# A fused FFT mixing and feed-forward kernel: its dense part put into program order on the compute engines, with a new order of issue

## The chip, the cores and the metric

One core of a Trainium2 chip. The metric is the device time of one launch in microseconds (us); lower is better. Each run of a kernel stands beside runs of the kernel before on the same chip, and all runs told here were in the fast state (no run was over 1.5% above the fastest of its kernel). The engines are named as in the profile: PE is TensorE, PEld its weight loads, DVE VectorE, ACT ScalarE, POOL GpSimd, SP SyncE.

## The reference

```python
def _attn_ref(x, filt_r, filt_i):                 # x: (8, 3008, 256)
    X = np.fft.rfft(x, axis=1)
    Y = X * (filt_r + 1j * filt_i)[None, :, :]
    return np.fft.irfft(Y, n=x.shape[1], axis=1).astype(np.float32)

def _moe_ref(x, w_in, w_out):                     # x: (24064, 256)
    h = x @ w_in                                  # 256 -> 2048
    g = h - np.tanh(h)
    return (g @ w_out).astype(np.float32)         # 2048 -> 256
```

The output of the first is the input of the second. Everything is fp32.

## The kernel before

A prologue transforms the first batch and prepares weights. Then comes the dense part: 48 groups of columns in five passes, each group in four *quarters*, 192 quarters in all. A quarter runs three stages at once, on different data: `up(U)` makes h for quarter U with seven half-size products in place of eight; `shrink(U-1)` turns h into h - tanh(h) by Arctan and Square, and makes four differences t on POOL; `down(U-2)` adds seven products into four accumulator banks. Between them run steps of the FFT of the next batch (`first`, `middle`: products pf, pz, pe). All eight PSUM banks are in use: x, y, z for `up`, t for the transforms, o0 to o3 for `down`.

```python
def up(U, between):
    ...
    mm(X, 1, True)
    s1 = copied("s1")                       # ACT copies bank x
    mm(Y, 2, True)
    between(0)
    V.tensor_add(h[:, 0, :, 0:w], Y, s1)
    mm(X, 6, False)                         # adds onto bank x: waits for the copy
    between(1)
    u2 = copied("u2")
    mm(Z, 5, True)
    between(2)
    mm(X, 7, False)
    u3 = copied("u3")
    between(3)
    V.tensor_add(h[:, 3, :, 0:w], Z, u3)
    mm(X, 4, False)
    between(4)
    V.tensor_copy(h[:, 2, :, 0:w], X)
    mm(Z, 3, False)                         # waits for the add above that reads bank z
    V.tensor_add(h[:, 1, :, 0:w], Z, u2)

def shrink(U):
    ...
    for k in (2, 0):                        # halves of h
        y[k], sq[k] = tiles("y", 2), tiles("sq", 1)
        ACT.activation(y[k], ht[k], AF.Arctan, scale=S)
        ACT.activation(y[k], y[k], AF.Square)
        yield
        V.tensor_mul(ht[k], ht[k], y[k])                       # "multiply"
        ACT.activation(sq[k], y[k], AF.Square, bias=near_b, scale=A)
        yield
        V.scalar_tensor_tensor(out=ht[k], in0=sq[k], scalar=K, in1=ht[k],
                               op0=ALU.add, op1=ALU.mult)      # "fused operation"
    t = dn.tile([128, 4, 2, 256], F32, tag="t", bufs=2, name="t")
    combine(blocks, [t[:, k, :, 0:w] for k in range(4)])       # four POOL subtractions
    ...

def down(U):
    ...
    mm(1, 2)
    if done:                                # last quarter of a group
        ACT.copy(p1, product(1))
        V.tensor_add(o[:, 0, 0:w], product(2), p1)
    yield
    ...                                     # mm(3, 5), mm(6, 7) likewise
    mm(4)
    if done:
        V.tensor_add(o[:, 1, 0:w], product(4), p1)
        store(i, o)                         # two DVE transposes, 32 stores

for U in range(total + 2):
    ...
    def between(k):
        if k < 4:
            next(dw, None)                  # a down step
        next(sh, None)                      # a shrink step
        ...                                 # transform steps that are due
```

Unless told otherwise, the program's scheduler reorders the instructions of each engine by its own simulated times; the order in the source is only a priority.

Of the kernel before, what the change touches and what calls it, by code (L numbers as in the profile page):

```python
# [22 lines left out]
NK = NQ // 2  # L23
# [11 lines left out]
XH = 2  # L35
# [10 lines left out]
def chunks_of(unit, size):  # L46
    n = steps_of(unit)
    return [(r, min(size, n - r)) for r in range(0, n, size)]
# [90 lines left out]
def kernel(  # L139
# [294 lines left out]

    hs, gs = {}, {}

    def up(U, between):

        i, u = divmod(U, 4)
        b, tu, w = uts[i]  # L440
        rhs = [b[0][0], b[1][0], b[1][1], tu[:, 3, 0:w], tu[:, 0, 0:w], tu[:, 1, 0:w],
               tu[:, 2, 0:w]]
        banks = {k: ps.tile([128, 2, 256], F32, tag=k, bufs=1, name=k) for k in "xyz"}
        X, Y, Z = (banks[k][:, :, 0:w] for k in "xyz")
        h = dn.tile([128, 4, 2, 256], F32, tag="h", bufs=3, name="h")
        hs[U] = (h, w)

        def mm(bank, q, first):
            for k in range(2):
                nc.tensor.matmul(bank[:, k], wu[:, q - 1, (2 * u + k) * 128:(2 * u + k + 1) * 128],  # L450
                                 rhs[q - 1], start=(first and k == 0), stop=True,
                                 skip_group_check=True)

        def copied(tag):
            t = dn.tile([128, 2, 256], F32, tag=tag, bufs=1, name=tag)[:, :, 0:w]
            ACT.copy(t, X)  # L456
            return t

        mm(X, 1, True)
        s1 = copied("s1")  # L460
        mm(Y, 2, True)
        between(0)
        V.tensor_add(h[:, 0, :, 0:w], Y, s1)  # L463
        mm(X, 6, False)
        between(1)
        u2 = copied("u2")
        mm(Z, 5, True)
        between(2)
        mm(X, 7, False)
        u3 = copied("u3")  # L470
        between(3)
        V.tensor_add(h[:, 3, :, 0:w], Z, u3)  # L472
        mm(X, 4, False)
        between(4)
        V.tensor_copy(h[:, 2, :, 0:w], X)  # L475
        mm(Z, 3, False)
        V.tensor_add(h[:, 1, :, 0:w], Z, u2)

    def shrink(U):

        h, w = hs.pop(U)
        ht = {k: h[:, k:k + 2].rearrange("p a b n -> p (a b) n")[:, :, 0:w] for k in (0, 2)}

        def tiles(tag, bufs):
            return dn.tile([128, 4, 256], F32, tag=tag, bufs=bufs, name=tag)[:, :, 0:w]

        y, sq = {}, {}
        for k in (2, 0):
            y[k], sq[k] = tiles("y", 2), tiles("sq", 1)
            ACT.activation(y[k], ht[k], AF.Arctan, scale=S)  # L490
            ACT.activation(y[k], y[k], AF.Square)  # L491
            yield
            V.tensor_mul(ht[k], ht[k], y[k])  # L493
            ACT.activation(sq[k], y[k], AF.Square, bias=near_b, scale=A)  # L494
            yield
            V.scalar_tensor_tensor(out=ht[k], in0=sq[k], scalar=K, in1=ht[k],  # L496
                                   op0=ALU.add, op1=ALU.mult)
        t = dn.tile([128, 4, 2, 256], F32, tag="t", bufs=2, name="t")
        blocks = [[h[:, 2 * a + k, :, 0:w] for k in range(2)] for a in range(2)]
        combine(blocks, [t[:, k, :, 0:w] for k in range(4)])  # L500
        gs[U] = (blocks, t, w)
        yield

    accs = {}

    def down(U):


        i, u = divmod(U, 4)
        b, t, w = gs.pop(U)  # L510
        rhs = [b[0][0], b[1][0], b[1][1], t[:, 3, :, 0:w], t[:, 0, :, 0:w], t[:, 1, :, 0:w],
               t[:, 2, :, 0:w]]
        if u == 0:
            accs[i] = [ps.tile([128, 2, 256], F32, tag=f"o{k}", bufs=1, name=f"o{k}")
                       for k in range(4)]
        acc = accs[i]
        at = {1: (0, 0), 2: (0, 1), 3: (1, 0), 5: (1, 1), 6: (2, 0), 7: (2, 1), 4: (3, 0)}

        def product(q):
            bank, k = at[q]  # L520
            return acc[bank][:, k, 0:w]

        def mm(*qs):
            for k in range(2):
                for q in qs:
                    nc.tensor.matmul(product(q), wd[:, q - 1, (2 * u + k) * 128:  # L526
                                                    (2 * u + k + 1) * 128],
                                     rhs[q - 1][:, k], start=(u == 0 and k == 0 and q == qs[0]),
                                     stop=(u == 3 and k == 1), skip_group_check=True)

        done = u == 3
        if done:
            p1, p5, u2, x12 = (dn.tile([128, 256], F32, tag=k, bufs=1, name=k)[:, 0:w]
                               for k in ("p1", "p5", "pu2", "x12"))
            o = dn.tile([128, 2, CH * 128], F32, tag="o", bufs=1, name="o")
        mm(1, 2)
        if done:
            ACT.copy(p1, product(1))
            V.tensor_add(o[:, 0, 0:w], product(2), p1)
        yield  # L540
        mm(3, 5)
        if done:
            ACT.copy(p5, product(5))
            V.tensor_add(x12, product(3), p5)
        yield
        mm(6, 7)
        if done:
            V.tensor_add(u2, product(6), p1)
            V.tensor_add(p1, product(7), u2)
            G.tensor_add(o[:, 0, w:2 * w], u2, x12)  # L550
            G.tensor_add(o[:, 1, w:2 * w], p1, p5)
        yield
        mm(4)
        if done:
            V.tensor_add(o[:, 1, 0:w], product(4), p1)
            accs.pop(i)
            store(i, o)
        yield

    def store(i, o):  # L560
# [116 lines left out]
    with tc.tile_pool(name="tr", bufs=2) as tr:  # L677
# [68 lines left out]
        with tc.tile_pool(name="dn", bufs=2) as dn, \  # L746
# [5 lines left out]
            for _ in last(0, z1):  # L752
                pass
            total = 4 * len(groups)
            for U in range(total + 2):
                i, u = divmod(U, 4)
                if U < total:
                    p, c = groups[i]
                    if c == 0 and u == 0:
                        units = 4 * len(CHUNKS[p])  # L760
                        steps, done = [], 0
                        if p + 1 < len(UNITS):
                            n_f = len(chunks_of(UNITS[p + 1], XH))
                            n_m = 2 * NK // (3 - len(UNITS[p + 1]))
                            steps = [(0.02 + 0.26 * k / n_f) * 4 * units for k in range(n_f)]
                            lo, hi = 0.34 * 4 * units, 4 * units - 14
                            steps += [lo + (hi - lo) * k / n_m for k in range(n_m)]
                            fs, ms = first(p + 1, z1), None
                    if u == 0 and i + 1 < len(groups) and c + 1 < len(CHUNKS[p]):
                        e2s[i + 1] = load_e2(*groups[i + 1])  # L770
                    if u == 2 and i + 1 < len(groups) and c + 1 == len(CHUNKS[p]):
                        e2s[i + 1] = load_e2(*groups[i + 1])
                    if u == 2 and i + 1 < len(groups):
                        lasts = last(i + 1, z1)
                sh = shrink(U - 1) if 0 <= U - 1 < total else iter(())
                dw = down(U - 2) if 0 <= U - 2 < total else iter(())

                def between(k):
                    nonlocal ms, done
                    if k < 4:  # L780
                        next(dw, None)
                    next(sh, None)
                    if U >= total:
                        return
                    if k < 4:
                        pos = 16 * c + 4 * u + k
                        while done < len(steps) and steps[done] <= pos:
                            if done < n_f:
                                next(fs)
                            else:  # L790
                                if ms is None:
                                    ms = middle(p + 1, z1)
                                next(ms)
                            done += 1
                    if u >= 2 and k in (1, 3) and i + 1 < len(groups):
                        next(lasts, None)
                    if i == len(groups) - 1 and k == 0:
                        next(bounds, None)

                if U < total:  # L800
                    if i == len(groups) - 1 and u == 0:
                        bounds = bounded(z1)
                    up(U, between)
                else:
                    for k in range(5):
                        between(k)

    within = nc.values_load(count[0:1, 0:1], min_val=0, max_val=128)
    with tc.If(within < 128):
# [33 lines left out]
```

## Time and profile before

| | before |
|---|---|
| time, median of 4 runs | 3037.57 us |
| prologue, dense part, tail | 206, 2807, 23 us |
| PE at its own spacing in the dense part | 2618 us |
| PE stalled in the dense part | 189 us |

The last two rows are the ones to read. The spacing is the distance from the start of one matmul record to the start of the next where nothing is waited for; whatever a distance is longer than that is a stall. Both are summed over the 12256 records of the dense part. Three rows of the costliest groups (line, engine, operation, tiles, shapes, count, then busy us, mean ns, and the idle time before):

```profile
L496 DVE SCALAR_TENSOR_TENSOR h<-sq,h 128x1024 f32<-128x1024 f32 (+2 forms) x384 | 474.7, 1236 | 181.5 <-ACT sq L494 175.5
L493 DVE TENSOR_TENSOR h<-h,y 128x1024 f32<-128x1024 f32 (+2 forms) x384 | 469.3, 1247 | 66.4 <-ACT y L491 64.1
...
L432 POOL TENSOR_TENSOR t<-t,h 128x512 f32<-128x512 f32 (+2 forms) x192 | 245.3, 1278 | 10.4
```

### The profile page before, as it was taken

What the parts mean: (1) busy time and instruction counts of PE and PEld (TensorE: products, weight loads), DVE (VectorE), ACT (ScalarE), POOL (GpSimd) and SP (SyncE); (2) the same over time, 40 slices, a digit from 0 to 9 for tenths busy, and PEclk for the clock granted to TensorE, in tenths of its full rate; (3) what the DMA queues carried; (4) which work ended last, traced back from release to release, by engine and by line L of the source; (5) the groups of instructions that cost most, each with busy time, mean ns of one, the idle gap of its engine ahead of it and who ended that gap; (6) DMA issues with size and microseconds to landing.
All of it is one profiled execution on the core that took longest, in us unless ns stands there. A gap on an engine that the chain in (4) does not pass through costs nothing.

```text
span 3035.6 us, 36258 instructions
## 1 busy us (share of the span) xinstructions
PE 2789.7 (92%) x12410; PEld 2261.0 (74%) x12410; DVE 1845.8 (61%) x2382; ACT 1822.8 (60%) x2432; POOL 1602.4 (53%) x1398
## 2 busy tenths in 40 slices
PE   2369999999999999999999999999999999999996
PEld 0247766887877777887877777788888878888886
DVE  4865565665655555665665565666666666666664
ACT  1336666666666666666666666656666666666563
POOL 4653676534465566554455565645455555544543
PEclk6569999999999999999999999999999999999998
DMA  9744343222222322222322222222122212110100
GB/s 165 268 119 131 98 117 109 80 75 80 74 69 57 76 78 60 65 61 83 86 58 61 69 74 61 69 60 61 44 50 57 73 46 51 32 27 14 21 8 15
DMA packets 328867, 220.32 MB, mean 73 GB/s; under 512 B 228305, under 2 KB 282581, under 8 KB 328322
## 3 DMA queue, kind: packets, MB, share of 16 engines
q1 hardware_dynamic: 272848, 151.84, 20.1%
q10 hardware_dynamic: 53202, 50.35, 5.5%
q0 software_dynamic: 2624, 15.73, 2.0%
q8 instruction: 100, 1.64, 0.2%
q14 instruction: 93, 0.76, 0.1%
HBM read 134.41 MB, written 83.36 MB: 72 GB/s over the span
## 4 chain that ended last, share of the span: by engine, by line
PE 76%; POOL 6%; ACT 5%; DVE 5%; DMA 4%; issue 3%; ACTq 0%; SPq 0%; POOLq 0%; DVEq 0%
PE o L526 32%; PE x L450 19%; PE z L450 9%; PE y L450 5%; PE pe L338 3%; PE pu L414 3%; PE pz L357 3%; POOL t L429 2%; PE pf L283 2%; DVE h L496 1%; POOL uv L374 1%; DMA ct<-a 1%; ACT sq L494 1%; DMA w<-in_moe_w_in_dram 1%; POOL o L550 1%
## 5 line engine op out<-in xcount | busy, mean ns | idle before, releaser
L526 PE MATMUL o<-t,wd 128*128 128x256 f32 (+2 forms) x3072 | 777.4, 375 | 0.5 <-POOL t L430 0.5
L429 POOL TENSOR_TENSOR t<-h 128x512 f32<-128x512 f32 (+2 forms) x192 | 239.3, 1246 | 847.0 <-DVE h L496 754.2
L526 PEld LDWEIGHTS o<-t,wd 128*128 128x128 f32 x3072 | 577.7, 190 | 77.9 <-issue 7.8
L490 ACT ACTIVATE y<-h 128x1024 f32<-128x1024 f32 (+2 forms) x384 | 385.1, 1032 | 384.4 <-DVE h L475 384.1
L450 PE MATMUL x<-tu,wu 128*128 128x256 f32 (+2 forms) x2304 | 593.8, 378 | 6.2 <-ACT u L456 6.0
L526 PE MATMUL o<-h,wd 128*128 128x256 f32 (+2 forms) x2304 | 585.5, 376 | 3.0 <-DVE h L496 2.9
L496 DVE SCALAR_TENSOR_TENSOR h<-sq,h 128x1024 f32<-128x1024 f32 (+2 forms) x384 | 474.7, 1236 | 181.5 <-ACT sq L494 175.5
L450 PEld LDWEIGHTS x<-tu,wu 128*128 128x128 f32 x2304 | 424.2, 190 | 157.2 <-issue 84.1
L493 DVE TENSOR_TENSOR h<-h,y 128x1024 f32<-128x1024 f32 (+2 forms) x384 | 469.3, 1247 | 66.4 <-ACT y L491 64.1
L526 PEld LDWEIGHTS o<-h,wd 128*128 128x128 f32 x2304 | 436.5, 191 | 60.0 <-DVE h L496 5.3
L494 ACT ACTIVATE sq<-y,near_b 128x1024 f32<-128x1024 f32 (+2 forms) x384 | 433.8, 1130 | 76.1 <-DVE h L496 71.6
L491 ACT ACTIVATE y<-y 128x1024 f32<-128x1024 f32 (+2 forms) x384 | 386.2, 1036 | 0.9
L456 ACT COPY u<-x 128x512 f32<-128x512 f32 (+2 forms) x384 | 219.7, 572 | 217.1 <-PE x L450 206.8
L463 DVE TENSOR_TENSOR h<-y,s 128x512 f32<-128x512 f32 (+2 forms) x192 | 130.3, 679 | 268.2 <-ACT s L456 206.2
L373 POOL TENSOR_TENSOR zs<-zs,ft 128x512 f32<-128x512 f32 x112 | 143.5, 1282 | 249.1 <-ACT zs L371 234.3
L450 PE MATMUL z<-ut,wu 128*128 128x256 f32 (+2 forms) x768 | 200.5, 382 | 65.2 <-DVE h L472 64.9
L432 POOL TENSOR_TENSOR t<-t,h 128x512 f32<-128x512 f32 (+2 forms) x192 | 245.3, 1278 | 10.4
L472 DVE TENSOR_TENSOR h<-z,u 128x512 f32<-128x512 f32 (+2 forms) x192 | 129.4, 674 | 194.9 <-ACT u L456 194.9
L430 POOL TENSOR_TENSOR t<-h,t 128x512 f32<-128x512 f32 (+2 forms) x192 | 239.7, 1249 | 0.0
L431 POOL TENSOR_TENSOR t<-h 128x512 f32<-128x512 f32 (+2 forms) x192 | 239.6, 1248 | 0.0
L450 PE MATMUL x<-ut,wu 128*128 128x256 f32 (+2 forms) x768 | 218.1, 408 | 11.1 <-DVE h L475 10.7
L450 PEld LDWEIGHTS z<-ut,wu 128*128 128x128 f32 x768 | 140.5, 190 | 100.8 <-DVE h L472 82.9
(96 smaller groups left out, 3360.5 us busy)
## 6 DMA issues: line engine op xcount, KB each, us to landing
a<-ct SPq DMA_DIRECT2D x64, 384.0 KB, 3.8
ct<-e ACTq DMA_DIRECT2D x128, 192.0 KB, 2.2
ft<-filt SPq DMA_DIRECT2D x48, 512.0 KB, 4.2
out_dram<-ot SPq DMA_DIRECT2D x1408, 16.0 KB, 1.5
x_sb<-in_x_dram SPq DMA_DIRECT2D x69, 256.0 KB, 2.8
ct<-a ACTq DMA_DIRECT2D x69, 256.0 KB, 2.7
e<-ct SPq DMA_DIRECT2D x33, 512.0 KB, 4.1
filt<-filt_sb POOLq DMA_DIRECT2D x2, 4096.0 KB, 16.1
```

Of the source, the lines that this page charges most:

```text
L429: G.tensor_sub(t[0], b[0][1], b[0][0])
L430: G.tensor_sub(t[1], b[1][1], t[0])
L431: G.tensor_sub(t[2], b[1][1], b[0][1])
L432: G.tensor_sub(t[3], t[1], b[1][0])
L450: nc.tensor.matmul(bank[:, k], wu[:, q - 1, (2 * u + k) * 128:(2 * u + k + 1) * 128], rhs[q - 1], start=(first and k == 0), stop=True, ski ...
L456: ACT.copy(t, X)
L490: ACT.activation(y[k], ht[k], AF.Arctan, scale=S)
L491: ACT.activation(y[k], y[k], AF.Square)
L493: V.tensor_mul(ht[k], ht[k], y[k])
L494: ACT.activation(sq[k], y[k], AF.Square, bias=near_b, scale=A)
L496: V.scalar_tensor_tensor(out=ht[k], in0=sq[k], scalar=K, in1=ht[k], op0=ALU.add, op1=ALU.mult)
L526: nc.tensor.matmul(product(q), wd[:, q - 1, (2 * u + k) * 128: (2 * u + k + 1) * 128], rhs[q - 1][:, k], start=(u == 0 and k == 0 and q == ...
```

## The change

Its intent: on each compute engine, work whose inputs are ready stands ahead of work that waits for a product of the running quarter; and PE, ACT, DVE and POOL then follow that order exactly (the program is told so by `tc.manual_schedule`; below this is called *forced*). Cut to its core:

```diff
-        mm(X, 1, True)
-        s1 = copied("s1")
-        mm(Y, 2, True)
-        between(0)
+        mm(X, 1, True)
+        mm(Y, 2, True)
+        s1 = copied("s1")
+        t(0); d(); s()                      # transform step, down products, shrink step
         V.tensor_add(h[:, 0, :, 0:w], Y, s1)
+        e(); s(); s(); t(1)                 # e: copies and adds of finished accumulators
         mm(X, 6, False)
-        between(1)
+        mm(Z, 5, True)
         u2 = copied("u2")
-        mm(Z, 5, True)
-        between(2)
+        d(); s(); e(); t(2)
         mm(X, 7, False)
         u3 = copied("u3")
-        between(3)
         V.tensor_add(h[:, 3, :, 0:w], Z, u3)
+        d(); s(); e(); t(3)
         mm(X, 4, False)
-        between(4)
         V.tensor_copy(h[:, 2, :, 0:w], X)
+        s(); d(); e(); t(4)
         mm(Z, 3, False)
         V.tensor_add(h[:, 1, :, 0:w], Z, u2)
@@ down
-            store(i, o)
+            stores.append((i, o))
@@ the loop over quarters
+            order = {nc.tensor.engine, ACT.engine, V.engine, G.engine}
+            with tc.manual_schedule(engines=order):
...
+                    def t(k):
+                        if k == 2 and stores:
+                            store(*stores.pop())      # one quarter later than before
...              # one transform step per slot, five slots per quarter
```

(Several calls are put on one line here; the shrink generator is split into six steps.)

More of the change, by code (lines that the diff above doesn't have):

```diff
@@ L435, with up @@
     hs, gs = {}, {}
-    def up(U, between):
+    def up(U, d, e, s, t):
         i, u = divmod(U, 4)
@@ L459, in up @@
         mm(X, 1, True)
+        mm(Y, 2, True)
         s1 = copied("s1")
-        mm(Y, 2, True)
-        between(0)
+        t(0)
+        d()
+        s()
         V.tensor_add(h[:, 0, :, 0:w], Y, s1)
+        e()
+        s()
+        s()
+        t(1)
         mm(X, 6, False)
-        between(1)
+        mm(Z, 5, True)
         u2 = copied("u2")
-        mm(Z, 5, True)
-        between(2)
+        d()
+        s()
+        e()
+        t(2)
         mm(X, 7, False)
         u3 = copied("u3")
-        between(3)
         V.tensor_add(h[:, 3, :, 0:w], Z, u3)
+        d()
+        s()
+        e()
+        t(3)
         mm(X, 4, False)
-        between(4)
         V.tensor_copy(h[:, 2, :, 0:w], X)
+        s()
+        d()
+        e()
+        t(4)
         mm(Z, 3, False)
@@ L487, in shrink, with start, square, end @@
         y, sq = {}, {}
-        for k in (2, 0):
-            y[k], sq[k] = tiles("y", 2), tiles("sq", 1)
+        def start(k):
+            y[k] = tiles("y", 2)
             ACT.activation(y[k], ht[k], AF.Arctan, scale=S)
             ACT.activation(y[k], y[k], AF.Square)
-            yield
+        def square(k):
+            sq[k] = tiles("sq", 1)
             V.tensor_mul(ht[k], ht[k], y[k])
             ACT.activation(sq[k], y[k], AF.Square, bias=near_b, scale=A)
-            yield
+        def end(k):
             V.scalar_tensor_tensor(out=ht[k], in0=sq[k], scalar=K, in1=ht[k],
                                    op0=ALU.add, op1=ALU.mult)
+        start(2)
+        yield
+        square(2)
+        yield
+        end(2)
+        yield
+        start(0)
+        yield
+        square(0)
+        yield
+        end(0)
         t = dn.tile([128, 4, 2, 256], F32, tag="t", bufs=2, name="t")
@@ L502, in shrink @@
         yield
-    accs = {}
+    accs, stores = {}, []
     def down(U):
@@ L536, in down @@
         mm(1, 2)
+        yield
         if done:
@@ L541, in down @@
         mm(3, 5)
+        yield
         if done:
@@ L546, in down @@
         mm(6, 7)
+        yield
         if done:
@@ L549, in down @@
             V.tensor_add(p1, product(7), u2)
+        yield
+        mm(4)
+        yield
+        if done:
+            V.tensor_add(o[:, 1, 0:w], product(4), p1)
             G.tensor_add(o[:, 0, w:2 * w], u2, x12)
             G.tensor_add(o[:, 1, w:2 * w], p1, p5)
-        yield
-        mm(4)
-        if done:
-            V.tensor_add(o[:, 1, 0:w], product(4), p1)
             accs.pop(i)
-            store(i, o)
+            stores.append((i, o))
         yield
@@ L754 @@
             total = 4 * len(groups)
-            for U in range(total + 2):
-                i, u = divmod(U, 4)
-                if U < total:
-                    p, c = groups[i]
-                    if c == 0 and u == 0:
-                        units = 4 * len(CHUNKS[p])
-                        steps, done = [], 0
-                        if p + 1 < len(UNITS):
-                            n_f = len(chunks_of(UNITS[p + 1], XH))
-                            n_m = 2 * NK // (3 - len(UNITS[p + 1]))
-                            steps = [(0.02 + 0.26 * k / n_f) * 4 * units for k in range(n_f)]
-                            lo, hi = 0.34 * 4 * units, 4 * units - 14
-                            steps += [lo + (hi - lo) * k / n_m for k in range(n_m)]
-                            fs, ms = first(p + 1, z1), None
-                    if u == 0 and i + 1 < len(groups) and c + 1 < len(CHUNKS[p]):
-                        e2s[i + 1] = load_e2(*groups[i + 1])
-                    if u == 2 and i + 1 < len(groups) and c + 1 == len(CHUNKS[p]):
-                        e2s[i + 1] = load_e2(*groups[i + 1])
-                    if u == 2 and i + 1 < len(groups):
-                        lasts = last(i + 1, z1)
-                sh = shrink(U - 1) if 0 <= U - 1 < total else iter(())
-                dw = down(U - 2) if 0 <= U - 2 < total else iter(())
-                def between(k):
-                    nonlocal ms, done
-                    if k < 4:
-                        next(dw, None)
-                    next(sh, None)
-                    if U >= total:
-                        return
-                    if k < 4:
-                        pos = 16 * c + 4 * u + k
-                        while done < len(steps) and steps[done] <= pos:
@@ new lines, with d, e, s @@
+            order = {nc.tensor.engine, ACT.engine, V.engine, G.engine}
+            with tc.manual_schedule(engines=order):
+                for U in range(total + 2):
+                    i, u = divmod(U, 4)
+                    if U < total:
+                        p, c = groups[i]
+                        if c == 0 and u == 0:
+                            units = 4 * len(CHUNKS[p])
+                            steps, done = [], 0
+                            if p + 1 < len(UNITS):
+                                n_f = len(chunks_of(UNITS[p + 1], XH))
+                                n_m = 2 * NK // (3 - len(UNITS[p + 1]))
+                                steps = [0.01 * units + 1.36 * units * k / n_f for k in range(n_f)]
+                                lo, hi = 1.6 * units, 5 * units - 17
+                                steps += [lo + (hi - lo) * k / n_m for k in range(n_m)]
+                                fs, ms = first(p + 1, z1), None
+                        if u == 0 and i + 1 < len(groups) and c + 1 < len(CHUNKS[p]):
+                            e2s[i + 1] = load_e2(*groups[i + 1])
+                        if u == 2 and i + 1 < len(groups) and c + 1 == len(CHUNKS[p]):
+                            assert done == len(steps)
+                            e2s[i + 1] = load_e2(*groups[i + 1])
+                        if u == 2 and i + 1 < len(groups):
+                            lasts = last(i + 1, z1)
+                    sh = shrink(U - 1) if 0 <= U - 1 < total else iter(())
+                    dw = down(U - 2) if 0 <= U - 2 < total else iter(())
+                    def d():
+                        next(dw, None)
+                    def e():
+                        next(dw, None)
+                    def s():
+                        next(sh, None)
+                    def t(k):
+                        nonlocal ms, done
+                        if k == 2 and stores:
+                            store(*stores.pop())
+                        if U >= total:
+                            return
+                        pos = 20 * c + 5 * u + k
+                        if u == 3 and k in (0, 2) and i + 1 < len(groups):
+                            next(lasts)
+                        elif done < len(steps) and steps[done] <= pos:
@@ L794, in between @@
                             done += 1
-                    if u >= 2 and k in (1, 3) and i + 1 < len(groups):
-                        next(lasts, None)
-                    if i == len(groups) - 1 and k == 0:
-                        next(bounds, None)
-                if U < total:
-                    if i == len(groups) - 1 and u == 0:
-                        bounds = bounded(z1)
-                    up(U, between)
-                else:
-                    for k in range(5):
-                        between(k)
+                        if i == len(groups) - 1 and k in (0, 2, 4):
+                            next(bounds, None)
+                    if U < total:
+                        if i == len(groups) - 1 and u == 0:
+                            bounds = bounded(z1)
+                        up(U, d, e, s, t)
+                    else:
+                        for k in range(5):
+                            s()
+                            s()
+                            d()
+                            e()
+                            t(k)
+                for w in stores:
+                    store(*w)
     within = nc.values_load(count[0:1, 0:1], min_val=0, max_val=128)
```

## The prediction

> **What bounds the kernel now.** I read the page first (engines, slices, chain), then busy time of the dense part alone, then the timeline of two short stretches, then the waits. "Dense part" is everything from the first product pu at 206.2 us to the last matmul at 3013 us.
>
> ```profile
> PE 2789.7 (92%) x12410; PEld 2261.0 (74%) x12410; DVE 1845.8 (61%) x2382; ACT 1822.8 (60%) x2432; POOL 1602.4 (53%) x1398
> ...
> PEclk6569999999999999999999999999999999999998
> ```
>
> TensorE (PE) is the engine to keep fed; the others are at 53 to 61%. Its clock is full from the third slice on, so what is lost later is not clock.
>
> ```profile
> 206.00:3013.00 2807.00, 2715.89 (x12256) 2222.27 (x12256) 1704.81 (x2040) 1771.93 (x2366) 1474.07 (x1278) 0.99 0.25 64
> ```
>
> So the prologue is 206, the dense part 2807 and the tail 23 us; the change touches only the dense part. Busy PE (second number) cannot be trusted to some 3%: ends of matmuls are modelled and run past the start of the next. A better measure is start to start:
>
> ```profile
> 999.78 1.67 PE L526 MATMUL o<-t,wd 128*128 128x256 f32 x7
> ...
> 1001.29 1.02 PE L357 MATMUL pz<-a,f 94*128 94x512 f32 x2
> ...
> 1002.16 1.03 PE L450 MATMUL x<-tu,wu 128*128 128x256 f32 x4
> ...
> 1004.80 1.05 PE L414 MATMUL pu<-s_sb,e 128*128 128x128 f32 x8
> ```
>
> (start, us, engine, line.) Each product is two records. Seven records of 256 columns begin at 999.78 and the next record at 1001.29: (1001.29-999.78)/7 = 0.216 us each; two of 512 columns take (1002.16-1001.29)/2 = 0.43. The end is modelled 0.16 late, so a pu record (128 columns) takes (1.05-0.16)/8 = 0.11. By the records of the dense part: 9632 of 256 columns in L450 and L526, x 0.216 = 2080; 1120 narrower ones there (0.163 or 0.189) 194; 384 of pz and pe with 512 and 128 with 256 columns 193; 756 pu 84; pf 72; the rest 3. Sum 2626; with unrounded spacings 2618. **So 2807-2618 = 189 us is all that reordering can win**, and 2850 us is the time with no stall at all.
>
> Where the 189 us are: I took every start-to-start distance less that floor. 108 us are in some hundred stalls over 0.25 us, of which 72 us (43 stalls) stand before the second product into bank z (z<-ut), 15 before x<-ut, 11 before x<-tu. The other 80 us are short ones, mostly 0.1 us: a weight load that had to wait and was not hidden; 313 of these (35 us) at x<-ut. The waits say the same:
>
> ```profile
> PEld z L450 <- DVE h L472: 82.9, 47, 3.6
> ...
> PE z L450 <- DVE h L472: 64.9, 40, 3.2
> PEld x L450 <- DVE h L475: 62.2, 153, 2.4
> ```
>
> (us in total, times, longest.) And one of the longest shows why:
>
> ```profile
> 985.98 0.71 DVE L569 STREAM_TRANSPOSE ot<-o 128x512 f32<-128x512 f32 x1 [4.35 <-POOL o L550]
> ...
> 986.61 0.65 DVE L472 TENSOR_TENSOR h<-z,u 128x512 f32<-128x512 f32 x1
> ...
> 987.32 1.13 PE L450 MATMUL z<-ut,wu 128*128 128x256 f32 x4 [3.16 <-DVE h L472]
> ```
>
> VectorE (DVE) stood 4.35 us before an output transpose that waited for GpSimd (POOL). Behind it, ready, was the add that frees bank z, and PE waited 3.16 us for that bank.
>
> **What the Trainium skill says.** "TensorE: Matmul & The Clock Gate", Architectural detail: only PE reorders, and only weight loads, pulled ahead of running matmuls; the other queues are strictly first in, first out. The stretch above agrees (4.35 us behind one transpose). Same page, "Wait — 56ns": spacing is N/2.4 GHz + 2.5 ns, 215.7 ns at N = 512; here 256 fp32 columns take 216 ns, so an fp32 record costs as twice its columns. "PSUM — Partial Sum Buffer", PSUM bank collisions: no two engines on one bank, reads included. The trace agrees: the DVE product uv waited 88.2 us (44 times) for ScalarE's (ACT) copies of the same bank. "Perfetto Trace Analysis", Identifying Dependency Chains: an instruction that waits for several engines may get a semaphore instruction ahead of it; here they took 51 ns on PE's weight queue (58 before pz), cheap.
>
> **The change, part by part.** No arithmetic is added or removed, so the 2618 us stay. (1) PE, ACT, DVE and POOL follow program order in the dense part, instead of an order chosen by the scheduler. (2) In each quarter (14 products up for U, shrink of U-1, 14 products down for U-2), mm5 moves ahead of the copy u2, and the down products stand between each write of bank X and the next. (3) Copies and adds of the finished accumulators (e) are a separate step; the transposes and stores wait until the third slot of the next quarter. (4) At most one transform step per slot, five slots per quarter; a step that meets the group's pu is put off.
>
> I lay out one plain quarter, t = 0 at mm1. PE: a product up 4 x 0.216 = 0.86, a down pair 1.73. mm1 0 to 0.86, mm2 to 1.73, down 1,2 to 3.46, mm6 to 4.32, mm5 to 5.18, down 3,5 to 6.91, mm7 to 7.78, down 6,7 to 9.50, mm4 to 10.37, down 4 to 11.23, mm3 to 12.1. An estimate from rows of the profile: ACT copy 0.58, Arctan and Square 1.05, second Square 1.15, DVE add or copy 0.68, multiply 1.27, fused one 1.26, and 0.2 from the last matmul's end to its reader.
> - ACT: s1 1.06-1.64, Arctan and Square 3.74, sq 4.89, u2 5.47, Arctan and Square 7.57, u3 (mm7 ready at 7.98) 8.56, sq 9.7.
> - DVE: h0 1.93-2.62, multiply 3.74-5.0, fused 6.33, h3 8.6-9.3, multiply 10.57, copy of X 11.25, fused 12.5, h1 13.2.
>
> Slack at each reuse: mm7 after u2 1.4 us, mm4 after u3 0.94, mm3 after h3 1.9, next mm1 after the copy of X 0.85, down 1,2 of the next quarter after the last fused one 1.3. POOL's four operations (5.1 us) end 5.5 us into the next quarter and are needed at 5.2 (t0, there at 1.7) to 10.4 (the last). **No wait is left in a plain quarter**, and the z wait and its 0.1 us restarts go.
>
> What stays, each an estimate by the same layout:
> - Start (no down, no shrink to fill) and drain: 6 + 8. The drain has an exposed chain add, activations, fused, POOL before as well.
> - First pass: 64 middle steps in some 72 consecutive slots. pz and pe share one bank: pz 0.86, 0.2, two ACT copies 1.16, DVE uv 0.7 make 3 us to the next step; where only one down pair of 1.73 lies between, PE waits. Laying out two neighbouring quarters with steps in all slots gave 0.7 and 0.9 us of stalls per 16.4; with restarts 1 us x 14.4 quarters = 15.
> - Later passes: 80 steps pz. At t0 one delays Arctan and so u2 and u3 (0.5 us), at t3 it delays the copy of X (0.25), else nothing: 80 x 0.15 = 12.
> - Each group's finishing quarter (two more DVE adds of 0.4 before the copy of X use up the 0.85): 48 x 0.15 = 7.
> - pu's weight loads and the bound check 8; waits for transfers where passes meet 4.
>
> Sum 60. Expected: 206 + 2618 + 60 + 23 = 2907, and +2 from the profiled execution (3035.6) to the median (3037.6): **2908 us**, -4.3%.
>
> **Rivals.**
> (a) In-order stalls take the place of the others: what had been moved past a waiting instruction now waits behind it, above all ACT and DVE behind a transform step or accumulator copy. For: ACT's queue also issues transfers, and in the first pass ACT carries 13 to 14 of 16.4 us. Against: ACT is at 63% (1772/2807) overall and all reuses have 0.85 us or more. If every quarter of passes 1 to 4 (168) lost 0.4 us more: +67, 2975.
> (b) POOL becomes the bound: 5.1 + 2.5 x 2.83 (zs, uv) + 1.2 = 13.4 of 16.4 us in the first pass. uv is used three slots later (some 10 us), so I expect little; 1 us per such quarter would be +14.
> (c) SyncE is still ordered by the scheduler: 32 stores of 0.43 us, 14 us per group, could hold up loads that PE now needs in a fixed order. Before, pf and pz lost under 3 us together. 48 groups x 0.5 us would be +24.
> (d) Nearly all stalls vanish: 2870 to 2880.
>
> **Range and chances.** The floor is 2850, nothing won is 3038. The layout says 60 us of stalls; I allow 25 to 115, so 2873 to 2963. 2% faster is 2977: stalls under 129 of now 189 us. Only (a) together with (c) reaches that. Faster 0.92, same 0.07, slower 0.01.
>
> **What would show it.** Right: the wait of z for the h add falls from 148 us (PE and PEld) to under 20, that of x for its copy from 73 to under 20; the transpose's 88.8 us wait for POOL is gone; records of PE and their spacing are unchanged; in the pass without transforms (after 2690 us before) PE runs at its floor, and the stalls left lie in the first pass. Wrong: PE waiting for ACT copies (u2, u3) or uv in the later passes, as in (a); PE waiting for transfers, as in (c); a longer prologue or tail; or a spacing other than 0.216.

## The result

2958.93 us (median of 4 runs, 2955.41 to 2963.86) against 3037.57 us: a ratio of 0.9741, 95% interval 0.9724 to 0.9759. Ratios here are the mean time of one kernel's runs over that of the other's in the same rounds, so not quite the ratio of the medians. The direction and the chances held and the time is inside the range, but near its slow end: 79 us were won of the 130 predicted, and the stalls, 115 us, are the very end of the 25 to 115 that the prediction allowed.

The stalls in the dense part, by pass (the first has the densest transforms, the last none):

| us | first | second | third | fourth | last | sum |
|---|---|---|---|---|---|---|
| before | 37.3 | 47.1 | 47.3 | 35.5 | 22.2 | 189 |
| predicted | 21 | 21 in these three | | | 18 | 60 |
| after | 42.5 | 16.8 | 20.4 | 16.5 | 18.5 | 115 |

(Predicted: first 15 + 6; middle three 12 + 4 + 5 of the 7 for finishing quarters; last 8 + 2 + 8.)

The waits of the changed kernel that answer to those shown for the one before (who waited for whom, us in total, times, longest); L480 is now the add that frees bank z, L486 the copy that frees bank x:

```profile
PEld x L450 <- DVE h L486: 35.2, 57, 1.3
...
PE x L450 <- DVE h L486: 12.8, 29, 0.9
...
PEld z L450 <- DVE h L480: 0.8, 3, 0.3
```

The z wait of 148 us is gone, as intended. The x wait fell only from 73 to 48 us. The page's rows of the multiply (L511), the fused operation (L515) and POOL's last difference tell what else happened:

```profile
L511 DVE TENSOR_TENSOR h<-h,y 128x1024 f32<-128x1024 f32 (+2 forms) x384 | 591.2, 1540 | 262.5 <-ACT y L507 262.4
...
L515 DVE SCALAR_TENSOR_TENSOR h<-sq,h 128x1024 f32<-128x1024 f32 (+2 forms) x384 | 565.4, 1472 | 20.8 <-DVE h L511 0.5
...
L432 POOL TENSOR_TENSOR t<-t,h 128x512 f32<-128x512 f32 (+2 forms) x192 | 306.9, 1598 | 0.0
```

The same instructions on the same shapes have become 0.29, 0.24 and 0.32 us longer. A stretch of the last pass, DVE and POOL only (start, duration, engine, line), shows them side by side:

```profile
2716.12 1.27 POOL L431 TENSOR_TENSOR t<-h 128x512 f32<-128x512 f32 x1
...
2716.29 2.18 DVE L511 TENSOR_TENSOR h<-h,y 128x1024 f32<-128x1024 f32 x1 [1.01 <-ACT y L507]
...
2717.36 2.25 POOL L432 TENSOR_TENSOR t<-t,h 128x512 f32<-128x512 f32 x1
...
2718.58 2.11 DVE L515 SCALAR_TENSOR_TENSOR h<-sq,h 128x1024 f32<-128x1024 f32 x1
...
2721.76 1.22 DVE L511 TENSOR_TENSOR h<-h,y 128x1024 f32<-128x1024 f32 x1
...
2723.73 1.22 DVE L515 SCALAR_TENSOR_TENSOR h<-sq,h 128x1024 f32<-128x1024 f32 x1
```

The engines take turns. The multiply at 2716.29 starts while POOL's subtraction runs to 2717.39, and takes 2.18 us instead of 1.22; POOL's next one starts at 2717.36 and takes 2.25 instead of 1.27, until after the multiply has ended at 2718.47; the fused operation at 2718.58 takes 2.11. Three microseconds later, with POOL idle, both take 1.22 us. PE itself loses nothing by it here: in the quarter of this stretch its stalls are 0.01 us. What the longer durations cost must be read from other quarters, and from runs 1 and 2. This is what the Trainium skill says in "SBUF — State Buffer", Who interferes with whom: "A DVE instruction with two SBUF inputs contends with a GpSimd instruction that reads SBUF". The page calls the shared port pair an exclusive lock, and the turns above look like one. I had not consulted it for the prediction.

From the starts and ends of all full-width instructions in the dense part I worked out which share of its time each had a POOL instruction beside it. For the multiply it went from 0.11 to 0.51, for the fused operation from 0.12 to 0.37. Without such company both took 1.22 us in both kernels; in the changed kernel, with POOL beside them for over 95% of their time, 1.88 and 2.01 us on average. An add that reads PSUM and one SBUF tile took 0.68 us either way.

### The profile page after: what moved, and what is told of

Read it like the earlier page. It is cut to its first block, busy times and chain, and to the rows that moved or that the text cites. A ratio compares the mean times of both kernels' runs of the same rounds, so it can differ in the third digit from the quotient of the medians.

```text
span 2958.8 us, 36473 instructions
## 1 busy us (share of the span) xinstructions
PE 2760.0 (93%) x12410; PEld 2278.3 (77%) x12410; DVE 2028.4 (69%) x2382; ACT 1863.2 (63%) x2432; POOL 1805.9 (61%) x1398
## 4 chain that ended last, share of the span: by engine, by line
PE 62%; DVE 9%; ACT 9%; POOL 7%; issue 5%; DMA 4%; SPq 3%; ACTq 1%; DVEq 0%; POOLq 0%
PE o L557 24%; PE x L450 16%; PE z L450 7%; PE y L450 4%; PE pe L338 3%; SPq L614 3%; PE pz L357 3%; DVE h L511 2%; PE pu L414 2%; ACT y L506 2%; POOL t L432 2%; PE pf L283 2%; DMA w<-in_moe_w_in_dram 1%; ACT y L507 1%; ACT u L456 1%
## 5 line engine op out<-in xcount | busy, mean ns | idle before, releaser
L511 DVE TENSOR_TENSOR h<-h,y 128x1024 f32<-128x1024 f32 (+2 forms) x384 | 591.2, 1540 | 262.5 <-ACT y L507 262.4
L515 DVE SCALAR_TENSOR_TENSOR h<-sq,h 128x1024 f32<-128x1024 f32 (+2 forms) x384 | 565.4, 1472 | 20.8 <-DVE h L511 0.5
L506 ACT ACTIVATE y<-h 128x1024 f32<-128x1024 f32 (+2 forms) x384 | 400.0, 1042 | 15.2 <-ACT e L341 7.2
L507 ACT ACTIVATE y<-y 128x1024 f32<-128x1024 f32 (+2 forms) x384 | 399.3, 1040 | 12.2
L456 ACT COPY s<-x 128x512 f32<-128x512 f32 (+2 forms) x192 | 110.9, 577 | 464.3 <-PE x L450 456.6
L432 POOL TENSOR_TENSOR t<-t,h 128x512 f32<-128x512 f32 (+2 forms) x192 | 306.9, 1598 | 0.0
L374 POOL TENSOR_TENSOR uv<-uv,zs 128x512 f32<-128x512 f32 x128 | 242.0, 1891 | 25.1 <-DVE uv L372 16.5
L373 POOL TENSOR_TENSOR zs<-zs,ft 128x512 f32<-128x512 f32 x112 | 166.3, 1484 | 142.5 <-ACT zs L371 142.4
L450 PE MATMUL x<-ut,wu 128*128 128x256 f32 (+2 forms) x768 | 201.1, 385 | 14.3 <-DVE h L486 12.8
L338 PE MATMUL pe<-uv,g 112*96 112x512 f32 (+1 forms) x320 | 149.0, 570 | 63.3 <-POOL uv L374 48.3
```

What stands on the lines that cost most here:

```text
L374: G.tensor_add(uv, uv, zs)
L432: G.tensor_sub(t[3], t[1], b[1][0])
L450: nc.tensor.matmul(bank[:, k], wu[:, q - 1, (2 * u + k) * 128:(2 * u + k + 1) * 128], rhs[q - 1], start=(first and k == 0), stop=True, ski ...
L456: ACT.copy(t, X)
```

## The experiments

Twelve runs, each beside runs of the kernel before (3034 to 3039 us by session). Profiles of the same kernel family differ by up to 8 us in the prologue (199 to 207 us), so for small differences I look at the stalls of the dense part.

| run | what | time, us | ratio to before | stalls, us |
|---|---|---|---|---|
| before | | 3037.57 | 1 | 189 |
| after | the change | 2958.93 | 0.9741 | 115 |
| 1 | change without POOL's differences (wrong) | 2929.33 | 0.9639 | 84 |
| 2 | change, differences replaced by fills (wrong) | 2923.45 | 0.9629 | 77 |
| 3 | before, program order forced | 3576.11 | 1.1763 | 729 |
| 4 | change, nothing forced | 2927.16 | 0.9642 | 82 |
| 5 | change, shrink steps earlier | 2938.15 | 0.9667 | 92 |
| 6 | as 5, second transform slot later | 2938.37 | 0.9673 | 94 |
| 7 | as 5, nothing forced | 2928.31 | 0.9633 | 83 |
| 8 | before, late stores | 3021.90 | 0.9942 | 179 |
| 9 | as 4, transposes pinned | 2883.34 | 0.9481 | 34 |
| 10 | change, only PE forced | 2952.50 | 0.9720 | 105 |
| 11 | change, ACT free | 2998.98 | 0.9877 | 153 |
| 12 | as 8, transposes pinned | 2930.57 | 0.9662 | 85 |

### Contention, or queue order (runs 1 and 2)

Theory A: the stalls beyond my 60 us come from DVE's two-input operations meeting POOL's reads. Theory B: they come from the fixed queues and from bank t.

Run 1:

```diff
-        t = dn.tile([128, 4, 2, 256], F32, tag="t", bufs=2, name="t")
-        combine(blocks, [t[:, k, :, 0:w] for k in range(4)])
-        gs[U] = (blocks, t, w)
+        gs[U] = (blocks, h, w)             # down reads h where it read t
```

> The changed kernel without the four GpSimd differences t of each quarter; the products down read h in their place, so the result is wrong on purpose. Theory A (contention): what is left of the stalls beyond my 60 us comes from VectorE's multiply and fused operation, which read two SBUF inputs and take longer while GpSimd reads SBUF (the Trainium skill, SBUF - State Buffer, Who interferes with whom). Then their means fall from 1.54 and 1.47 to 1.30 or less, the stalls of the dense part from 115 to 75 us or less, and the time from 2959 to 2920 or less. Theory B (queue order and shared bank): slower VectorE work lies in the slack, and the stalls are waits for ScalarE copies and for bank t. Then the means fall too, but the time stays above 2945.

Run 2:

```diff
-        combine(blocks, [t[:, k, :, 0:w] for k in range(4)])
+        for k in (0, 1, 2, 3, 0, 1, 2, 3):
+            G.memset(t[:, k, :, 0:w], 0.5)
```

> As the changed kernel, but the four differences t are eight GpSimd fills of the same tiles, which read nothing (wrong result on purpose). GpSimd stays busy and still hands t to TensorE. Theory A: it is GpSimd's reads that slow VectorE, so multiply and fused operation fall to 1.30 us or less, as without the operations, and the time to within 10 us of that run. Rival: GpSimd's writes or its occupancy count, and both VectorE means stay above 1.40 us.

Run 1, the two DVE rows:

```profile
L511 DVE TENSOR_TENSOR h<-h,y 128x1024 f32<-128x1024 f32 (+2 forms) x384 | 482.1, 1255 | 261.9 <-ACT y L507 261.9
L515 DVE SCALAR_TENSOR_TENSOR h<-sq,h 128x1024 f32<-128x1024 f32 (+2 forms) x384 | 482.0, 1255 | 20.5 <-ACT e L341 0.5
```

Run 2, the same rows, and POOL's fills:

```profile
L511 DVE TENSOR_TENSOR h<-h,y 128x1024 f32<-128x1024 f32 (+2 forms) x384 | 486.4, 1267 | 262.1 <-ACT y L507 261.9
...
L515 DVE SCALAR_TENSOR_TENSOR h<-sq,h 128x1024 f32<-128x1024 f32 (+2 forms) x384 | 487.7, 1270 | 20.4 <-ACT e L341 0.5
...
L532 POOL MEMSET t<- 128x512 f32 (+2 forms) x1536 | 712.0, 516 | 170.4 <-PE o L558 170.3
```

POOL is busy with 712 us of writes in run 2, beside the multiply for 116 us and beside the fused operation for 167 us of them, and DVE is as fast as without them: it is the reads. The stalls fall from 115 to 84 and 77 us and the time by 30 and 35 us. Theory B, which had the time above 2945, falls as the main cause. Theory A's own thresholds (75 us, 2920) were just missed: contention carries some 31 to 38 us of the 55 us that I had not predicted, not all of them. The two runs also take away or shorten POOL's own work (1036 us of differences), and with it PE's waits for t; those cannot be the main part, since the stalls before o<-t were 7 us in the changed kernel, while those before the products into x, a bank that DVE and ACT free, fell from 58 to 37 and 36 us.

### Which part of the change does it (runs 3, 4, 10, 11)

Run 3 puts the loop of the kernel before into `tc.manual_schedule` for the four engines and leaves its order alone.

> The kernel before with program order forced on the four engines, its emission order untouched. If the forced order alone is the gain, under 2990 us. I expect the opposite: the old program has the add of Z next to the copy it waits for and the second product into Z straight behind the down products, transposes ahead of the adds, so every wait stands in the queue: 3150 us or more (each of 192 quarters losing 0.6 us more).

It took 3576 us with 729 us of stalls, 289 of them before the second product into z. The direction was expected; the size (2.8 us per quarter over 192 quarters, not 0.6) was not. The old source order was never meant to be followed; the scheduler had been repairing it.

Run 4 is the other half:

```diff
-            with tc.manual_schedule(engines=order):
+            if True:
```

> The changed program with no forced order: the scheduler arranges the new emission order. If the emission order (priorities) is the gain, 2975 or less. If forcing is needed, 3000 to 3040, with the z waits for the h add back above 80 us.

Here I was wrong, and it is the main surprise: with one line of the change taken back the kernel is 32 us *faster* than with it. The new emission order alone is worth more than the whole change. Unforced, the scheduler runs the first Arctan before the copy s1. In the changed kernel s1 stands ahead of it in ACT's queue, though s1 waits for this quarter's first product and the Arctan's input is ready: ACT waits 456.6 us before s1 there. It is the very thing that the change set out to avoid. With Arctan earlier, the fused operation and so POOL's reads come earlier in the quarter, and fall beside DVE work that reads PSUM (the differences ran beside it for 212 us in the changed kernel and for 256 us in run 4): the means of the two DVE operations are 1.33 and 1.31 us in run 4.

Run 10 forces PE alone, run 11 forces all but ACT.

> The new emission order with program order forced on TensorE alone. If the 32 us that forcing costs lie in the queues of ScalarE, VectorE and GpSimd, this stays near the unforced one: 2920 to 2935. If TensorE's own fixed order costs them, 2950 or more.

> The changed kernel with ScalarE's order free and the other three forced. If ScalarE's queue (s1, waiting for a product of this quarter, ahead of a ready Arctan; its wait for x before s1 is 457 us) carries the cost of forcing, this gains 20 us or more on 2959. If VectorE's order sets when GpSimd begins, and with it the contention, ScalarE alone gains little: 2945 or more.

Both went against what I hoped. By its own test (2950 us or more) run 10 lays a cost on PE's own order. Fixing PE's order alone brings 22 us of stalls back (82 to 105), 13 of them in the first pass (26.6 to 39.8), though the two DVE means stay at 1.33 and 1.32 us; so the cost of forcing is not only contention. The traces say where these 13 us lie: before product pe, whose stalls in the first pass are 10 us in run 4 and 24 us in run 10 (6 before the change, 20 with it). pe writes bank t, which DVE's product uv must have read first; PE stood 8.2 us (4 times) for that in run 4 and 19.7 us (17 times) in run 10. In run 10 the order puts between pz and pe one down pair at seven places (6.2 us of stalls there) and mm4 with the last down product at six (13.3 us); in run 4 the scheduler has put one more product up between them at all thirteen, and 8.9 us are left. With ACT free and the rest forced the stalls are 153 us, more than with all forced, and ACT waits 194 us for DVE before its second Square: its order was chosen for other queues than it got. Contention is no smaller there either: the two DVE means are 1.47 and 1.55 us, and the third and fourth difference take 1.76 and 1.79 us. So the costs of single queues do not add up; run 11's was not traced further.

### Moving the shrink steps (runs 5, 6, 7)

Run 5 keeps the forced order and mends the place just named:

```diff
+        s()                    # Arctan, Square of U-1: ready before this quarter
         mm(X, 1, True)
         mm(Y, 2, True)
         s1 = copied("s1")
...
         d(); s(); e()
+        s()                    # last fused operation and POOL's differences, before mm7
         t(2)
         mm(X, 7, False)
```

(the later shrink calls are dropped).

> The changed kernel, order still forced, with the shrink steps earlier in the quarter: the first Arctan and Square ahead of the copy s1 (their input is ready before this quarter's first product), and the last fused operation ahead of the product mm7, so that GpSimd's differences begin some 4 us earlier in the quarter. Theory A, made precise: in the changed kernel the emission puts s1, which waits for a product of this quarter, ahead of a ready Arctan; that pushes the fused operation late, so GpSimd's reads fall on VectorE's next multiply and fused operation. Then here both means fall to 1.30 us or less with GpSimd's reads all in place, the stalls to 75 us, the time to 2925 or less. Rival B: forced queues cost the time whatever the order (waits for bank t, stores); then no better than 2945.

> As the run before it, and the second transform slot stands behind product mm6 and its copy u2, so that the steps pz and pe, which share bank t, have 2.6 us of other matmuls between them and not 1.73. If bank t is what is left in the first pass (32 us of stalls there with GpSimd's reads taken away, 20 of them before pe and before mm7), this takes 8 to 15 us more off. If not, the two runs agree within 4 us.

> The early-shrink order without forcing. If the emission order sets the time and the scheduler adds only local swaps: within 10 us of the forced one. If the scheduler still finds 20 to 30 us that a forced order cannot: 2905 or less.

Run 5 won 21 us, not 34. The fused operation fell to 1.29 us, but the multiply only to 1.47. By the starts and ends in its trace one of a quarter's two multiplies takes 1.56 us, the other 1.38. What runs beside the slower one is to a half POOL's work for the transforms (uv and zs, 102 of 205 us of overlap) and only for 33 us the last difference t. So the differences were moved off DVE's way, but they were not all that stood in it. Run 6 gave nothing: the first pass has 34.8 us of stalls, against 34.7 in run 5. But this does not refute that pz and pe follow too closely there. At the seven places whose distance it lengthened the stalls before pe fell from 5.1 to 0.3 us, and at the other places they rose from 9.4 to 16.0: the wait moved. One of these distances became shorter by the same edit; why the others rose was not traced. Run 7 equals run 4 within 2 us: once the scheduler may swap locally, my rearrangement adds nothing.

### The transposes (runs 8, 9, 12)

Run 4 still lost 82 us, 31 of them before x<-ut. Before its transposes DVE waited longer than in the kernel before (the kernel before, then run 4):

```profile
DVE ot L569 <- POOL o L550: 88.8, 44, 4.4
...
DVE ot L604 <- POOL o L589: 111.0, 45, 4.2
```

One of the longest stalls (run 4, the engines in order of time):

```profile
1634.80 0.72 POOL L589 TENSOR_TENSOR o<-pu,x 128x256 f32<-128x256 f32 x1
...
1635.55 0.71 DVE L604 STREAM_TRANSPOSE ot<-o 128x512 f32<-128x512 f32 x1 [4.20 <-POOL o L589]
1636.19 0.65 DVE L486 COPY h<-x 128x512 f32<-128x512 f32 x1
...
1636.89 0.80 PE L450 MATMUL x<-ut,wu 128*128 128x256 f32 x1 [3.13 <-DVE h L486]
```

It is the picture of the kernel before again: DVE stands 4.2 us before a transpose that waits for POOL, with the copy that frees a bank behind it, and PE waits 3.1 us for that bank. The source has the transposes a quarter later, but the scheduler had moved them forward to where its simulation took their input as ready. Run 8 shows the same in the kernel before: late stores in the source, and DVE still waited 79 us before the transposes.

> The kernel before with one part of the change alone: the output transposes and stores of a finished group wait until the third step of the next quarter. In the kernel before VectorE stood 89 us before these transposes, 44 times, with the add that frees bank z behind it in many cases. I expect the stalls before z to fall from 77 to about 40 us and the time to 2995 to 3010. If the transposes only hide another wait, no change (3030 or more).

The gain was 17 us over the kernel before in the same session, which is under the 2% that count as faster here, and about half of what I expected: the transposes had not stayed where the source put them. Runs 9 and 12 pin them to their place in DVE's order:

```diff
-            V.transpose(ot[:, h, 0:total], o[:, h, 0:total])
+            tc.keep_in_program_order(V.transpose(ot[:, h, 0:total], o[:, h, 0:total]))
```

> The new emission order unforced (2927 us), with one thing pinned: the output transposes keep their place behind the fused operation of the next quarter. Unforced, the scheduler moved them forward again; VectorE stood 111 us (45 times) before them for GpSimd, and 24 us of TensorE's stalls stood behind that, before x in the second quarter of a group. If that is the cause, these 24 us go, and the time is 2900 to 2912. If another wait comes in their place, 2920 or more.

> The kernel before with the late transposes of the earlier run, now pinned to their place. Without the pin the scheduler had moved them forward again (VectorE still stood 79 us, 42 times, before them). If the transposes in VectorE's queue are the largest single cause in the kernel before, the wait before them goes to nothing, the stalls fall by as much as the pin took from the new order (48 us, from 82 to 34), and the time is 2975 to 2992. If the old emission order is the larger cause, 3005 or more.

Run 9, the transposes and what DVE waited for before them:

```profile
L604 DVE STREAM_TRANSPOSE ot<-o x96: 529/684/712, 299.1 to 2860.1; 128x512 f32<-128x512 f32 x86, 128x384 f32<-128x384 f32 x6, 128x448 f32<-128x448 f32 x4
its engine sat idle before it (us, times) until:
who waited for it (us, times):
```

The first list is empty (the few entries of the second are left out). The stalls fell from 82 to 34 us, twice the 24 that I could point to, and the time to 2883.34 us: 5.2% under the kernel before and the fastest correct version. By pass its stalls are 16.4, 2.9, 4.3, 2.0 and 8.1 us. Run 12, the kernel before with its stores a quarter later and pinned, takes 2930.57 us: a few lines beat the whole change. I had expected 2975 us at best; its stalls fell by 104 us against the kernel before, and by 94 against run 8, not by 48. The wait before z, 77 us of stalls in the kernel before, is 0.9 us there.

## Why the prediction was right or wrong

- **The floor.** Right. The changed kernel has the same 12256 records; their median spacing is 0.216 us, the prologue 204 and the tail 23 us. All but 2 of the 77 us between the two profiles came out of the 189 us. (206 + 2618 + 60 + 23 + 2 is 2909 and not 2908.)
- **The z wait and the transposes.** Right. The wait on the add of z fell from 148 to 0.8 us, the wait of the transposes on POOL's o from 89 to 19. The other two signs of being right failed: the x wait is 48 us and not under 20, and 42.5 of the 115 us of stalls lie in the first pass, not most of them.
- **"No wait is left in a plain quarter".** Nearly so, but not by the layout that it was read from. The durations in it, "multiply 1.27, fused one 1.26", were read from a kernel in which POOL ran beside them a tenth of the time, and taken as constants. My own layout had POOL's four differences running from the last fused operation to 5.5 us into the next quarter, and the next multiply and fused operation from 3.74 to 6.33: the overlap stood in my numbers and I did not see it. Measured, the full-width instructions took 1.57 and 1.49 us on average. Yet the 27 quarters with no matmul of a transform or of the bound check in or just before them lost 4.2 us together, 3.0 of these in three quarters of the last pass. In such a quarter the first multiply and fused operation took 2.14 and 1.82 us, but the second multiply, which stands before the copy of x, took 1.21: the slack was there where the durations were wrong. To that extent it was luck.
- **The sum of 60 us.** Here is the step that failed: what is added in quarters that carry more than the plain one. It measured 115. In the first pass (21 predicted, 42.5 measured) 20 us stand before product pe, the wait for bank t that the term of 15 us was meant for, and 12 in the first two quarters, pu included, where 6 were expected. In the middle passes (21 predicted, 53.7 measured) some 24 us stand before x<-ut, for DVE's copy of x, and 20 before x<-tu, which waits for ACT's copies u2 and u3; the layout had 0.25 and 0.5 us for these, at single steps. Contention explains 31 to 38 of the 55 us missing, by runs 1 and 2: without it the middle passes lose some 33 us and the first 32. Of the rest, what the fixed order of PE adds before pe is shown by runs 4 and 10; the other part stays open. The last pass (18 against 18.5) is right in its sum and partly by luck: the drain cost 3 us and not 8.
- **The rivals.** (a) had the right form, forced queues cost something, but blamed ACT and DVE waiting in line; freeing ACT alone made it worse, and fixing PE alone already brings back 22 of the 33 us of stalls that forcing all four adds to run 4. (b) POOL as a bound: no; it went from 53 to 61% busy, through contention. (c) loads held up by stores: not seen; after the first pu, PE's matmuls waited for a transfer once, 2.8 us. That the two engines slow each other was in no rival. (d) nearly no stalls, 2870 to 2880 us: only run 9 comes near, with 2883.
- **Range and chances.** The time is inside, 4 us from the upper end. "Faster" at 0.92 was justified; the margin came from the size of the z wait, which was sure to go.

## What to carry to other kernels

First find the one instruction that blocks an in-order queue for something that isn't urgent: pinning the transposes behind ready work (run 12, 104 us under the kernel before of its session) won more than reordering everything by hand and forcing it (79 us). A good source order may be worth more as a hint than as a law; try it both ways before you keep the forcing, and look at what a fixed order forbids: here one more product between pz and pe. And when an order changes, durations change with it: list which instructions of VectorE read two SBUF tiles and lay GpSimd's work beside the others.

## What the Trainium skill lacked or had wrong

- "SBUF — State Buffer", Who interferes with whom: right, and it was my omission. It gives no size for the two-input case. Here a VectorE multiply of 128x1024 fp32 took 1.22 us alone and 1.88 us with GpSimd beside it nearly throughout, the fused operation 1.22 and 2.01; a GpSimd subtraction took up to 2.28 instead of 1.27. GpSimd fills, which only write, left both VectorE means at 1.27 us, as the page says.
- "TensorE: Matmul & The Clock Gate", Back-to-back issue gap and Wait — 56ns: neither says how many records of a profile an fp32 product makes, or their spacing. Here one of 256 columns is two records of 0.216 us each, and each has the value that the page gives for one matmul of 512 columns.
- "Perfetto Trace Analysis", Identifying Performance Opportunities (Optimization Strategy): consistent bubbles "can mean" too few buffers. Here 77 us of repeated stalls before one PSUM bank went to 0.9 us with the same buffers, by moving a group's two transposes, with their stores, in an in-order queue and pinning them there (run 12); the page doesn't name that cause.
